# Linear attention with a mixture of depths: TensorE's warm-up in 32 products of 192 columns instead of 12 of 512, each fill of 512 columns as two of 256

## The chip, the cores and the metric

The kernel runs on one core of a Trainium2 chip. The metric is the device time of one execution in microseconds, as the median of several runs. The trace is of one execution that the hardware profiler recorded.

## The reference

Eight batches of eight heads go through an attention whose softmaxes are taken separately over q's features and over k's sequence. The result feeds a layer that picks 128 of 576 rows per batch by a score, sends them through two matrix products with a relu between, and adds them back, scaled by a gate.

```python
def _attn_ref(q, k, v):                      # each (8, 8, 576, 64): B, H, S, D
    q_s = np.exp(q - np.max(q, axis=-1, keepdims=True))
    q_s = q_s / (np.sum(q_s, axis=-1, keepdims=True) + 1e-09)
    k_s = np.exp(k - np.max(k, axis=2, keepdims=True))
    k_s = k_s / (np.sum(k_s, axis=2, keepdims=True) + 1e-09)
    kv = np.einsum('bhsd,bhse->bhde', k_s, v)
    return np.einsum('bhsd,bhde->bhse', q_s, kv)
# x: the result as (B, S, H*D) = (8, 576, 512); w1 (512, 1024), w2 (1024, 512), capacity 128
def _moe_ref(x, w_gate, w1, w2, capacity):
    scores = np.einsum('bsd,d->bs', x, w_gate)
    out = x.copy()
    for b in range(B):
        top_idx = np.argpartition(-scores[b], capacity)[:capacity]
        xe = x[b, top_idx]
        ye = np.maximum(xe @ w1, 0.0) @ w2
        g = 1.0 / (1.0 + np.exp(-scores[b, top_idx]))
        out[b, top_idx] = xe + g[:, None] * ye
    return out
```

## The kernel before, in words

The work of the attention is cut into 16 units: a unit is one batch and four of its eight heads. For a unit, `load` brings k, v and q to the core (three buffers each), `k_exp` and `q_exp` take exponentials on ScalarE, `v_copy` (L275) copies v beside a column of ones, `kv_mm` (L311; `kv_mm_parts`, L299, for unit 1) forms the products of exponentials and v on TensorE, `kv_out` (L319 to L323) divides them on VectorE, `q_t` (L340, L347) turns q by TensorE, with copies back to the core's memory at L350 and L352, and `x_mm` (L375, with fillers of bf16 at L364) forms the unit's rows x. `x_sums` and `x_scale` (L386 to L393) divide them and `x_store` writes them out.

For a batch, `score_row` (L432) spreads its scores, `compare` (L443) ranks them on VectorE, and the chosen rows go through the two products with w1 and w2: `mlp1` (L555) and `mlp2` (L564) for the first two batches, and for pairs of later ones a scheme with fewer products of half the size (L648, L704). Batch 0's rows are taken by products with a selection matrix (`select`, L504 to L509), the others by an indirect load.

The order of all of this is written out by hand: each engine executes its instructions in the order in which the kernel issues them, and the pieces of the two products are spread between the units (`pieces`, `upto`). Ahead of the first unit there is no work for TensorE while the first loads are under way.

In that place the kernel issues products that nobody reads, with `ones_b` (128x512 bf16 ones) as both operands. The warm-up (L174) is 12 products of 512 columns into one bank of the accumulation memory, right after VectorE has set `ones_b`. `fill(n)` (L854) issues n such products into a bank of the tag "mm". It is called four times, all at the head of the kernel: fill(1) after the products at L860, which spread w_gate, and ahead of `kv_mm(0)`; fill(3) between `kv_out(0)` and `q_t(0, 0)`; fill(1) ahead of `x_mm(0, 0)`; fill(1) ahead of `q_t(1, 1)`. Each product is two instructions of TensorE, a load of its stationary operand (PEld in the profile) and the product (PE). A product of two f32 operands is issued as two such pairs, and each of them is counted as one product in the profile.

At the end eight more products of the same kind stand (L1177), and a branch that skips a general path.

Of the kernel before, what the change touches and what calls it, by code (L numbers as in the profile page):

```python
# [17 lines left out]
def kernel(  # L18
# [23 lines left out]
    nc = tc.nc  # L42
    B, H, S, D = q.shape
    DM, F = moe_w1.shape
    P = 128
# [15 lines left out]
    NV = 5  # L61
    TURNED = frozenset((11, 13, 15))
    HC = 32
    WARM = 12
    assert S == 64 * T and D == 64 and DM == H * D and DM == 512 and H % 4 == 0
    assert 1 < capacity < S and KF == 8 and NQ == 2
    assert B * S <= 32 * 256
# [14 lines left out]
    def bank(tag, bufs):  # L82
        return ps.tile([P, 512], F32, tag=tag, name=tag, bufs=bufs)
# [84 lines left out]
    ones_b = const.tile([P, 4 * P], BF16, name="ones_b")  # L168
    nc.vector.memset(ones_b, 1.0)
    w_ps = bank("tp", 2)  # L170
    ones_f = const.tile([1, D], F32, name="ones_f")
    nc.vector.memset(ones_f, 1.0)
    for n in range(WARM):
        nc.tensor.matmul(out=w_ps, lhsT=ones_b[:, :P], rhs=ones_b, start=True, stop=True)  # L174
    warm = const.tile([P, 1], F32, name="warm")
    nc.scalar.activation(out=warm, in_=ones_b[:, :1], func=AF.Exp)
    ident = const.tile([P, P], F32, name="ident")
# [672 lines left out]
    def fill(n):  # L850

        junk_ps = bank("mm", 2)
        for _ in range(n):
            nc.tensor.matmul(out=junk_ps, lhsT=ones_b[:, :P], rhs=ones_b, start=True, stop=True)  # L854


    wg = const.tile([P, NQ, 2, D], F32, name="wg")
# [1 line left out]
    for h in range(2):  # L859
        nc.tensor.matmul(out=g_ps[part(h), :4 * D], lhsT=ones_f,  # L860
                         rhs=w_row.rearrange("o (n i x) -> o i n x", i=2, x=2 * D)[:, h], start=True, stop=True)
    fill(1)
    ready(0)
    nc.vector.tensor_copy(out=wg.rearrange("p a i d -> p (a i d)"), in_=g_ps[:, :4 * D])
    kv_mm(0)
    q_exp(0, 0)
    q_exp(0, 1)
    kv_out(0)
    fill(3)

    q_t(0, 0, on_vector=True)
# [6 lines left out]
    q_exp(1, 1)  # L878
    k_exp(1)
    fill(1)  # L880
    x_mm(0, 0)
    x_mm(0, 1)
# [323 lines left out]
```

## Time and profile before

| what | us |
|---|---|
| median of three runs | 198.19 |
| the three runs | 197.4, 198.19, 198.81 |
| the profiled execution | 197.7 |
| its span, first to last instruction | 195.8 |
| TensorE busy, products | 184.2 |
| VectorE busy | 130.4 |
| ScalarE busy | 99.7 |
| GpSimd busy | 72.7 |

Times in the profile are counted from the start of the span. A product's recorded duration holds its way through the engine, and products overlap, so the distance between the starts of two is what one costs in a run of them.

### The profile page before, as it was taken

What the parts mean: (1) busy time and instruction counts of PE and PEld (TensorE: products, weight loads), DVE (VectorE), ACT (ScalarE), POOL (GpSimd) and SP (SyncE); (2) the same over time, 40 slices, a digit from 0 to 9 for tenths busy, and PEclk for the clock granted to TensorE, in tenths of its full rate; (3) what the DMA queues carried; (4) which work ended last, traced back from release to release, by engine and by line L of the source; (5) the groups of instructions that cost most, each with busy time, mean ns of one, the idle gap of its engine ahead of it and who ended that gap; (6) DMA issues with size and microseconds to landing.
All of it is one profiled execution on the core that took longest, in us unless ns stands there. A gap on an engine that the chain in (4) does not pass through costs nothing.

```text
span 195.8 us, 7049 instructions
## 1 busy us (share of the span) xinstructions
PE 184.2 (94%) x2927; PEld 156.0 (80%) x2927; DVE 130.4 (67%) x429; ACT 99.7 (51%) x160; POOL 72.7 (37%) x131
## 2 busy tenths in 40 slices
PE   5798899999999999999999999999999999999990
PEld 2466699894679996769999888899998889898860
DVE  6377966494669749928978989489959955444010
ACT  3474625658199759938675759365423133312100
POOL 8013551100860392099682312242314354701230
PEclk9999999999999999999999999999999999999997
DMA  5999999999999999989999799989451514010011
GB/s 153 364 365 378 378 368 364 328 388 352 341 379 374 336 314 363 308 248 152 312 325 320 130 317 330 273 160 257 158 121 57 121 38 149 32 54 5 3 56 63
DMA packets 48361, 46.67 MB, mean 238 GB/s; under 512 B 16321, under 2 KB 41921, under 8 KB 48322
## 3 DMA queue, kind: packets, MB, share of 16 engines
q1 hardware_dynamic: 46768, 41.62, 67.4%
q0 software_dynamic: 1280, 4.20, 6.7%
q8 instruction: 25, 0.41, 0.9%
q10 hardware_dynamic: 274, 0.33, 0.5%
q14 instruction: 14, 0.11, 0.2%
HBM read 34.61 MB, written 11.53 MB: 236 GB/s over the span
## 4 chain that ended last, share of the span: by engine, by line
PE 85%; DVE 6%; DMA 3%; issue 1%; ACT 1%; POOL 1%; POOLq 0%; DVEq 0%
PE mm L704 19%; PE mm L648 18%; PE tp L311 10%; PE x L375 10%; PE mm L555 8%; PE mm L564 8%; PE x L347 4%; DMA v<-in_v_dram 3%; PE mm L509 2%; PE tp L432 2%; PE x L530 2%; DVE xs L393 1%; DVE v_ones L280 0%; PE tp L468 0%; DVE v_ones L275 0%
## 5 line engine op out<-in xcount | busy, mean ns | idle before, releaser
L443 DVE SCALAR_TENSOR_TENSOR junk<-srow,s,stairs 128x576 bf16<-128x576 f32 x40 | 33.4, 834 | 1.5 <-ACT srow L435 0.8
L393 DVE TENSOR_TENSOR xs<-x,qrec 128x640 f32<-128x640 f32 x32 | 25.2, 815 | 0.0
L375 PE MATMUL x<-kv_w,qT 64*64 64x66 f32 x1152 | 23.2, 222 | 1.2 <-issue 0.5
L375 PEld LDWEIGHTS x<-kv_w,qT 64*64 64x64 f32 x1152 | 20.7, 134 | 4.5 <-issue 2.1
L352 ACT COPY qT<-x 128x512 f32<-128x512 f32 (+1 forms) x24 | 14.3, 643 | 17.1 <-PE x L347 16.6
L311 PE MATMUL tp<-v_ones,ke 128*64 128x65 f32 x600 | 21.6, 224 | 1.4 <-DVE v_ones L275 1.1
L704 PE MATMUL mm<-w,hT 128*128 128x256 f32 x96 | 22.2, 379 | 0.0
L249 ACT ACTIVATE ke<-k 128x1280 f32<-128x1280 f32 x16 | 20.4, 1274 | 3.4 <-issue 1.4
L311 PEld LDWEIGHTS tp<-v_ones,ke 128*64 128x64 f32 x600 | 19.2, 137 | 3.6 <-issue 1.9
L493 POOL DMA_INDIRECT xr<-out_dram,idx x8 | 8.1, 1018 | 36.3 <-DVE no L486 9.8
L704 PEld LDWEIGHTS mm<-w,hT 128*128 128x128 f32 x96 | 17.8, 190 | 2.2
L257 ACT ACTIVATE qe<-q 128x640 f32<-128x640 f32 (+1 forms) x26 | 16.4, 683 | 5.7 <-DMA q<-in_q_dram 3.0
L704 PE MATMUL mm<-tw,hT 128*128 128x256 f32 (+1 forms) x80 | 17.6, 363 | 0.0
L648 PE MATMUL mm<-xT,w 128*128 128x128 f32 x144 | 17.5, 276 | 0.0
L275 ACT COPY v_ones<-v 128x1280 f32<-128x1280 f32 x12 | 15.1, 1258 | 3.8 <-PE tp L311 2.5
L648 PEld LDWEIGHTS mm<-xT,w 128*128 128x128 f32 x144 | 16.8, 192 | 0.1
L555 PE MATMUL mm<-xT,w 128*128 128x128 f32 x128 | 16.7, 281 | 0.0
L713 POOL TENSOR_TENSOR o<-o,xr 128x256 f32<-128x256 f32 x9 | 6.8, 757 | 23.6 <-ACT o L712 23.6
L564 PE MATMUL mm<-w,hT 128*128 128x512 f32 x32 | 15.6, 611 | 0.0
L555 PEld LDWEIGHTS mm<-xT,w 128*128 128x128 f32 x128 | 15.0, 191 | 0.5
L704 PEld LDWEIGHTS mm<-tw,hT 128*128 128x128 f32 x80 | 13.8, 190 | 2.0 <-DVE o L717 0.4
L386 DVE RECIPROCAL qrec<-x 128x10 f32<-128x10 f32 x32 | 7.0, 217 | 12.6 <-PE x L375 12.2
(162 smaller groups left out, 311.2 us busy)
## 6 DMA issues: line engine op xcount, KB each, us to landing
q<-in_q_dram SPq DMA_DIRECT2D x26, 288.0 KB, 5.7
v<-in_v_dram SPq DMA_DIRECT2D x16, 320.0 KB, 5.4
out_dram<-xs SPq DMA_DIRECT2D x16, 320.0 KB, 5.6
k<-in_k_dram SPq DMA_DIRECT2D x15, 320.0 KB
k<-in_k_dram SPq DMA_DIRECT2D x16, 256.0 KB, 5.9
v<-in_v_dram SPq DMA_DIRECT2D x16, 256.0 KB
out_dram<-xs SPq DMA_DIRECT2D x16, 256.0 KB, 4.8
w<-in_moe_w_dram SPq DMA_DIRECT2D x4, 512.0 KB, 8.2
```

Source lines behind the costliest of these rows:

```text
L249: nc.scalar.activation(out=ke, in_=raw["k"][u % LD], func=AF.Exp)
L257: nc.scalar.activation(out=st["qe", u][:, r0:r1], in_=qr[:, r0:r1], func=AF.Exp)
L275: copy(out=v_ones[:, :, :, :D], in_=raw["v"][u % LD])
L311: nc.tensor.matmul(out=kv[part(h), i], lhsT=ke[:, 2 * h + i, r], rhs=vo[:, 2 * h + i, r], start=(r == 0), stop=(r == N2))
L352: nc.scalar.copy(out=to, in_=src)
L375: nc.tensor.matmul(out=to[:, r * C:(r + 1) * C], lhsT=lhsT, rhs=kw[part(i), a], start=True, stop=True)
L393: nc.vector.tensor_mul(xs[b][:, :, qd, :, a].rearrange("p r i d -> p i r d"), x[:, :, :, :D], rec.to_broadcast([P, 2, R, D]))
L443: nc.vector.scalar_tensor_tensor(junk, st["srow", b], st["s", b][:, r:r + 1], not_before[r], op0=OP.subtract, op1=OP.is_ge, accum_out=st[" ...
L555: nc.tensor.matmul(out=h_ps[:, f % HT * m:(f % HT + 1) * m], lhsT=w1[:, d, f * P:(f + 1) * P], rhs=xT[:, d, :m], start=(d == 0), stop=(d = ...
L564: nc.tensor.matmul(out=st["y", b][:m], lhsT=st["hT", b][:, f // HT, f % HT, :m], rhs=w2[:, f], start=(f == 0), stop=(f == KF - 1))
L648: nc.tensor.matmul(out=out_ps[:, f * m:(f + 1) * m], lhsT=w[:, k, f * P:(f + 1) * P], rhs=x()[:, k], start=first and f == 0 and k == 0, st ...
L704: nc.tensor.matmul(out=ps_of[to][:m, c:c + step], lhsT=st["hT", a][:, n, f, :m], rhs=w[:, f, c:c + step], start=first and f == 0, stop=f = ...
```

## The change

`WARM` is 32 instead of 12, and each of these products has 192 columns instead of 512: 6,144 columns in either case. `fill(n)` issues 2n products of 256 columns instead of n of 512. In all there are 20 products more in the warm-up and 6 more in the fills, 26 products or 52 instructions. Nothing else differs.

```diff
--- before.py
+++ after.py
@@ -61,7 +61,7 @@
     NV = 5
     TURNED = frozenset((11, 13, 15))
     HC = 32
-    WARM = 12
+    WARM = 32
     assert S == 64 * T and D == 64 and DM == H * D and DM == 512 and H % 4 == 0
     assert 1 < capacity < S and KF == 8 and NQ == 2
     assert B * S <= 32 * 256
@@ -171,7 +171,7 @@
     ones_f = const.tile([1, D], F32, name="ones_f")
     nc.vector.memset(ones_f, 1.0)
     for n in range(WARM):
-        nc.tensor.matmul(out=w_ps, lhsT=ones_b[:, :P], rhs=ones_b, start=True, stop=True)
+        nc.tensor.matmul(out=w_ps[:, :192], lhsT=ones_b[:, :P], rhs=ones_b[:, :192], start=True, stop=True)
     warm = const.tile([P, 1], F32, name="warm")
     nc.scalar.activation(out=warm, in_=ones_b[:, :1], func=AF.Exp)
     ident = const.tile([P, P], F32, name="ident")
@@ -850,8 +850,8 @@
     def fill(n):
 
         junk_ps = bank("mm", 2)
-        for _ in range(n):
-            nc.tensor.matmul(out=junk_ps, lhsT=ones_b[:, :P], rhs=ones_b, start=True, stop=True)
+        for _ in range(2 * n):
+            nc.tensor.matmul(out=junk_ps[:, :2 * P], lhsT=ones_b[:, :P], rhs=ones_b[:, :2 * P], start=True, stop=True)
 
 
     wg = const.tile([P, NQ, 2, D], F32, name="wg")
```

## Rows read from the trace of the kernel before

**Rows 1.** The page: part 1's line of TensorE (busy us, share of the span, instructions; loads are PEld), part 3's line of its instruction queue (packets, MB, share of 16 engines), and part 4, the chain that ended last, by engine.

```profile
PE 184.2 (94%) x2927; PEld 156.0 (80%) x2927; DVE 130.4 (67%) x429; ACT 99.7 (51%) x160; POOL 72.7 (37%) x131
...
q8 instruction: 25, 0.41, 0.9%
...
PE 85%; DVE 6%; DMA 3%; issue 1%; ACT 1%; POOL 1%; POOLq 0%; DVEq 0%
```

**Rows 2.** The chain of work that ended last, in order of time, from 2 to 11 us: start us, us, what, and how many instructions.

```profile
2.32 5.13 DMA v<-in_v_dram
...
7.54 0.84 DVE v_ones L275
...
8.51 1.39 PE tp L311 x40
9.90 0.75 PE mm L854 x3
10.65 0.47 PE x L347 x10
```

**Rows 3.** The timeline of TensorE's products from 0 to 13 us, instructions of one kind merged: start us, us until the last one ends, then in brackets the idle time before and what ended it.

```profile
2.07 4.45 PE L174 MATMUL tp<-ones_b 128*128 128x512 bf16 x12 [2.07 <-DVE second_p L182]
6.45 0.65 PE L860 MATMUL tp<-w_row,ones_f 1*64 1x256 f32 x4
7.03 0.39 PE L854 MATMUL mm<-ones_b 128*128 128x512 bf16 x1
8.51 1.39 PE L311 MATMUL tp<-v_ones,ke 128*64 128x65 f32 x40 [1.09 <-DVE v_ones L275]
9.83 0.82 PE L854 MATMUL mm<-ones_b 128*128 128x512 bf16 x3
10.58 0.77 PE L347 MATMUL x<-ident,qe 64*128 64x64 f32 x18
...
12.03 0.73 PE L375 MATMUL x<-kv_w,qT 64*64 64x66 f32 x33 [0.35 <-DVE qT L350]
```

**Rows 4.** The table by stretches: us from the span's start, length, then busy time and instructions of PE, PEld, DVE, ACT and POOL, the granted clock, the DMA share and GB/s.

```profile
2.00:4.00 2.00, 1.93 (x5) 0.74 (x6) 1.64 (x13) 1.17 (x1) 1.93 (x5) 1.00 0.73 211
```

**Rows 5.** Line L174, the warm-up: its loads with their duration (ns min/median/max), and single loads and a product from the timeline (start us, us).

```profile
L174 PEld LDWEIGHTS <-ones_b x12: 97/152/152, 2.1 to 5.9; 128*128 128x128 bf16 x12
...
5.04 0.15 PEld L174 LDWEIGHTS <-ones_b 128*128 128x128 bf16 x1 [0.28 <-issue]
5.46 0.56 PEld L174 LDWEIGHTS <-ones_b 128*128 128x128 bf16 x3 [0.27 <-issue]
...
5.93 0.10 PEld L174 LDWEIGHTS <-ones_b 128*128 128x128 bf16 x1
...
6.14 0.38 PE L174 MATMUL tp<-ones_b 128*128 128x512 bf16 x1
```

**Rows 6.** What one product costs: two long stretches of the chain (36 products of 256 columns, 64 of 128; start us, us), and the five loads of 128x128 bf16 at L477, whose products have 5 columns, together in the timeline.

```profile
150.22 8.04 PE mm L704 x36
...
167.15 7.38 PE mm L648 x64
...
29.23 0.19 PEld L477 LDWEIGHTS <-hit 128*128 128x128 bf16 x5
```

**Rows 7.** The chain in order of time: the pieces called issue that lie inside TensorE's work: the four longest, and one short one.

```profile
17.16 0.23 issue
...
23.63 0.39 issue
...
36.31 0.25 issue
...
50.31 0.06 issue
...
138.36 0.14 issue
```

**Rows 8.** The table by stretches with the columns of rows 4, cut where TensorE resumes after the stops called issue: first from one such point to the next, then from the start to one of them and to two earlier points. In brackets behind the second and the third time are the numbers of products and of loads.

```profile
17.37:24.01 6.64, 5.45 (x125) 4.62 (x126) 5.35 (x15) 3.57 (x7) 4.20 (x11) 1.00 1.05 382
24.01:36.55 12.54, 12.29 (x252) 11.64 (x252) 6.85 (x30) 6.29 (x8) 3.30 (x5) 1.00 1.04 355
36.55:138.48 101.93, 101.67 (x1905) 85.52 (x1904) 78.13 (x256) 68.16 (x108) 42.52 (x75) 1.00 0.98 300
...
0.00:24.01 24.01, 18.71 (x345) 12.58 (x346) 16.50 (x66) 12.47 (x18) 8.98 (x27) 1.00 0.94 327
...
0.00:15.93 15.93, 12.26 (x194) 7.21 (x196) 10.01 (x44) 8.16 (x11) 4.78 (x16) 1.00 0.88 300
0.00:20.63 20.63, 16.29 (x320) 10.62 (x322) 13.47 (x58) 9.85 (x13) 7.09 (x24) 1.00 0.92 319
```

**Rows 9.** The timeline from 15 to 31 us: start us, us, what, and in brackets the idle time before.

```profile
16.70 0.46 PE L375 MATMUL x<-kv_w,qT 64*64 64x66 f32 x15 [0.23 <-DVE krec L286]
...
20.22 0.80 PE L311 MATMUL tp<-v_ones,ke 128*64 128x65 f32 x20
...
21.61 0.77 PE L340 MATMUL x<-ident,qe 128*128 128x128 f32 x5 [0.58 <-ACT qe L257]
...
22.69 0.94 PE L509 MATMUL mm<-hT,xs 128*128 128x128 f32 x6
...
25.09 0.29 DVE L504 TENSOR_TENSOR hT<-slot_no,rank 128x128 f32<-128x128 f32 x1
```

## The prediction

> **What bounds the kernel now.** I read the page's share of the chain first, then the chain in order of time, then TensorE's timeline. TensorE is busy 94% of the span and carries 85% of the chain that ended last [rows 1]; from about 24 us on, its queue is full and nearly everything that delays it delays the end. Ahead of that the chain runs through a load: the first v lands at 7.45, VectorE copies it until 8.38, and only then does TensorE begin the first kv products, at 8.51 [rows 2]. The warm-up and the first fill lie beside that wait: TensorE is through with them at 7.42 and stands idle for 1.09 us [rows 3]. So the reader is to see two different places in one edit: the warm-up and fill(1) at 7.03 have a cover, and fill(3) at 9.83 has none, since the chain steps from L311 through L854 into L347 [rows 2]. The third call, fill(1) after the transposes, is covered again: the L375 products behind it wait 0.35 us for VectorE's qT [rows 3]. The fourth lies between x_mm and the transposes of unit 1.
>
> **The clock at the start.** The granted clock stands at 1.00 in the first stretches [rows 4], yet eight warm-up products follow each other at 0.43 us (5.04, 5.46, and so back to the first: 8 x 0.42 us is the 3.39 from 2.07 to 5.46), which is 512 columns at 1.2 GHz, and the later ones at 0.21 (5.93, 6.14), which is 2.4 GHz [rows 5]. I trust the spacings: TensorE ran at the lower level from 2.07 to 5.46, with products back to back, and then rose.
>
> **The warm-up.** The columns are the same, 6,144. If a weight load hides behind the product before it, as it does at 512 columns (it takes 0.15 us of 0.43 [rows 5]), the lower level fits 3.39 / 0.16 = 21 products of 192 columns, and the other 11 take 0.08 each: the end stays at 6.45. What does one more product cost by itself? In long stretches 36 products of 256 columns take 8.04 us, 223 ns each, and 64 of 128 columns take 7.38 us, 115 ns each [rows 6]. Two halves therefore cost 231 ns where one whole costs 223: some 7 ns for the extra pair of instructions. The upper bound is a bf16 load of 128 columns with a product of 5, where nothing hides anything: five loads take 0.19 us in all [rows 6], one takes 0.10 [rows 5], so they follow at 24 ns, 48 at half the clock. With that, a cold product takes 0.208 us, 16 of them fit into 3.39 us, and 16 more at 0.104 end at 7.1 instead of 6.45. The four L860 products and fill(1) still end by about 8.1, ahead of 8.51. Cost: nothing on the path, at either bound; the cover is the landing of v. If the cover were gone, it would be 0.14 us (20 x 7 ns) to 0.7 us.
>
> **The fills.** fill(3) is six products of 256 for three of 512: 3 x 7 = 0.02 us, upper bound 3 x 24 = 0.07. From the first of the three to L347 there are 0.75 us [rows 3]; two distances of 0.21 [rows 5] leave 0.32 from the last one to L347, where a product takes 0.21. If that 0.32 is a fixed delay from the start of the last product, the shorter last product cannot shrink it, and fill(3) grows by up to 0.1. So the bounds are 0 and 0.17; I take 0.02, the long stretches being the nearest rows. The first and the third call cost nothing, by their covers; the fourth has one pair more, 0.01 at most 0.02.
>
> **The 52 instructions as a shift.** This is where I expect the only visible effect. The chain has four stops of TensorE called issue, in the middle of runs of equal products, with nothing waited for: 0.23 at 17.16, 0.39 at 23.63, 0.25 at 36.31 and 0.14 at 138.36 [rows 7]. Between the instructions at which it resumes stand 251, 504 and 3,809 products and loads [rows 8], which are 1, 2 and 15 lots of 251 to 254 (waits of the sequencer are not in these counts). A cause tied to the data would not keep to such a lattice: I read them as points at equal counts of TensorE's instruction stream, and the page's instruction queue moves in 25 transfers of 0.41 MB, some 16 KB each [rows 1]. The Trainium skill, Runtime: NRT & Kernel Launch, section Instruction fetch mechanics, says that engines refill their instruction memory in blocks of 256 instructions; the counts agree with it.
>
> If so, all stops come 52 instructions earlier in the work than before. I look each up by its count:
> - The second stood at 345 + 346 = 691; 639 is close to 20.63, where the count is 642 [rows 8]. That is within the second half of kv_mm(2), L311, which ends some 0.6 us before the transposes L340, and these wait 0.58 us for ScalarE's qe [rows 9]. So 0.39 us leaves the path. What is late next: the products of L509 need VectorE's hits, of which the fourth is finished at 25.38 [rows 9]; without the stop TensorE, eight products for each hit and 0.115 us a product from 22.69 on, would want it at 25.45, so the feed just about keeps up. I take -0.39, bounds -0.45 and 0.
> - The first stood at 691 - 251 = 440; 388 is at 15.9, where the count is 390 [rows 8]: in L299, the kv products of unit 1. The L375 products behind them wait at 16.70 for VectorE's krec [rows 9], which reads what L299 makes. Either VectorE's own queue hides the stop there (-0.23), or krec comes late by as much as TensorE had stood still before (0). A longer stop there would be a loss: I take 0, bounds -0.23 and +0.16, the difference to the longest.
> - The third and the fourth move by 26 products too, in or just ahead of the run of short products in which they stood; I have no reason for another price and take 0 for each. They are worth 0.39 together [rows 7].
> - 5,854 products and loads [rows 1] hold some 23 such points; nineteen showed no stop of size, and each may get one. A shift by 26 products leaves most of them in a run of the same kind as before, so I don't take the rate of 4 in 23 for all of them, but one new stop of 0.25 at 4 chances in 10: +0.1. Bounds: 0, and two of the largest, 0.78.
>
> **The sum.** The profiled execution took 197.7 us, span 195.8 and 1.9 around it. 0 + 0.02 - 0.39 + 0 + 0.1 gives about -0.3, so 197.4. The median of the runs is 198.19, 0.49 above this execution; on that footing the forecast is 197.9.
>
> **Rivals.** (a) Nothing moves: the shift is worth zero because the stops are hidden in most executions or reappear at the same price. For it: 19 of 23 points had none. Then 198.2. The same section of the Trainium skill says that crossing a block is mostly hidden; by it the sum would lose the -0.39 and stand at 198.3, and the trace disagrees at four places, with 0.14 to 0.39 us. (b) Stops get worse: the new points fall where TensorE has little queued, as in the short products of L311 at 50.3, where a trace of one is seen already (0.06 [rows 7]). Two stops of 0.39 more and none less: 198.2 + 0.8 = 199.0. (c) Slower: 192-column products do not raise the clock as 512-column ones did. Place: L174, up to the first L311. It decides if products still come at the half rate when L311 starts at 8.51. Up to there the cover holds even then (32 x 0.16 ends at 7.19, the L860 products and the fill at about 8.7). From then on the chain's TensorE pieces up to 11.15 double: 1.39 + 0.75 + 0.47 = 2.6 us more [rows 2], and 0.2 for the late start: 201.0. Against it: weights load in 0.15 us at the lower level and a product of 192 takes 0.16, so nothing should open a gap. (d) The edit does not do what it says: the repeated load of equal weights might be left out by the build. In the trace each product has its own load (12 and 12 [rows 3, 5]), so I give this little; it would give 198.2 as in (a).
>
> **How the numbers follow.** Forecast 0.45, (a) with (d) 0.30, (b) 0.15, (c) 0.06, and 0.04 for a larger gain from a cause that I don't see (all four stops together hold only 1.0 us). The runs of before lie between 197.4 and 198.81, so 1%, or 2 us, is about what a measurement tells from no change. The range: down by all four stops from 198.2 and 0.5 for the spread, 196.7; up to (b) and a little spread, 199.2; (c) is left out. Faster by over 1% (under 196.2) is that last case: 0.04. Slower by over 1% (over 200.2) is (c) and little else: 0.07. Within 1%: 0.89.
>
> **What would show it.** Right: 32 L174 products at 0.16 and later 0.08 us, ending near 6.45; L311 still starting about 8.5 after v; L854 at 9.83 with six products in about 0.75 us; no issue stop inside L509, and L509's last start some 0.4 us nearer to L340's. Stops, where there are any, again at counts 251 to 254 apart, 52 earlier in the work. Wrong: L174 at 0.2 us or more with L311 later than 8.5; the stop still inside L509 at the same product; half-rate spacings after 8.5.

## The result, and the profile after

| | before | changed |
|---|---|---|
| median, 23 runs each | 198.94 us | 200.36 us |
| all runs | 197.33 to 201.84 | 198.6 to 205.49 |
| ratio | | 1.0062, 95% interval 1.0034 to 1.0089 |

The medians are of all executions, while every ratio here leaves out those of either kernel that fell into a slower state. The change costs some 1.2 us where 0.3 us of gain was forecast, and 200.36 lies above the range of 196.7 to 199.2. The profiled execution of the changed kernel took 204.06 us, well above its median, so the losses in it are larger than the usual ones; the profile of the third experiment below, at 200.7 us, shows the same places at a more usual size.

The page of the changed kernel: span, busy times, the granted clock by slices, and the chain by engine.

```profile
span 202.2 us, 7101 instructions
...
PE 186.7 (92%) x2953; PEld 161.6 (80%) x2953; DVE 130.6 (65%) x429; ACT 99.3 (49%) x160; POOL 73.0 (36%) x131
...
PEclk9999759999999999999999999999999999999998
...
PE 81%; DVE 9%; issue 3%; DMA 3%; ACT 1%; POOLq 0%; POOL 0%; DVEq 0%
```

TensorE has more to do by 2.5 us only, and its share of the chain falls from 85% [rows 1] to 81%, while issue rises from 1% to 3% and VectorE from 6% to 9%. The clock line has a dip in the fifth and sixth slice, from 20.2 to 30.3 us. The start is as the prediction had it, in the timeline of TensorE's products (start us, us, idle before):

```profile
2.08 4.53 PE L174 MATMUL tp<-ones_b 128*128 128x192 bf16 x32 [2.08 <-DVE second_p L182]
6.54 0.65 PE L860 MATMUL tp<-w_row,ones_f 1*64 1x256 f32 x4
...
8.63 1.39 PE L311 MATMUL tp<-v_ones,ke 128*64 128x65 f32 x40 [1.13 <-DVE v_ones L275]
9.95 0.83 PE L854 MATMUL mm<-ones_b 128*128 128x256 bf16 x6
10.71 0.77 PE L347 MATMUL x<-ident,qe 64*128 64x64 f32 x18
...
20.08 0.68 PE L311 MATMUL tp<-v_ones,ke 128*64 128x65 f32 x14
23.03 0.59 PE L311 MATMUL tp<-v_ones,ke 128*64 128x65 f32 x6 [2.27 <-issue]
23.55 1.33 PE L340 MATMUL x<-ident,qe 128*128 128x128 f32 x5
```

The warm-up of 32 ends at 6.54 where 12 had ended at 6.45 [rows 3]; L311 waits for v at 8.63, with 1.13 us to spare; the six products of fill(3) take 0.76 us to L347 where the three took 0.75. The loss is in the last rows. L311's second half stops after 14 of 20 products and goes on 2.27 us later. TensorE's waits name this stop and a second one:

```profile
PE tp L432 <- issue: 2.4, 1, 2.4
PE tp L311 <- issue: 2.3, 1, 2.3
```

Here is the table by stretches (length, products and loads in brackets, the granted clock third from the end), cut where TensorE goes on after these two stops and after a wait of 0.9 us in L468 (put down to VectorE's L393), and from the start to the first of them:

```profile
16.34:23.02 6.68, 4.26 (x126) 3.56 (x126) 5.51 (x20) 3.12 (x5) 3.52 (x10) 0.98 1.05 384
23.02:78.80 55.78, 53.34 (x1010) 45.26 (x1010) 33.92 (x128) 31.69 (x48) 20.09 (x36) 0.94 1.01 338
78.80:107.29 28.49, 27.57 (x509) 22.03 (x509) 21.61 (x68) 20.88 (x33) 15.34 (x21) 1.00 0.89 248
...
0.00:23.02 23.02, 16.82 (x346) 13.88 (x347) 15.77 (x64) 11.29 (x16) 8.30 (x26) 0.99 0.93 327
```

Between the resumptions stand 252, 2,020 and 1,018 products and loads: 1, 8 and 4 lots of 252 to 255, as in [rows 8]. The first resumption is at count 346 + 347 = 693, where before the stop in L509 stood at 691 [rows 8]. The same count of the stream lies 26 products earlier in the work, in L311. So the stops are where I put them, but one that was to vanish has grown sixfold. What follows it, with the two other pieces of the chain that matter (start us, us, what):

```profile
23.00:27.00 4.00, 3.97 (x26) 3.40 (x26) 3.86 (x15) 1.18 (x2) 2.73 (x4) 0.50 1.07 366
...
25.50 6.61 PE mm L509 x40
...
77.78 1.03 issue
```

After the stop the granted clock of 23 to 27 us is 0.50, the 1.2 GHz level; TensorE had stood still for 2.27 us. L509's 40 products take 6.61 us, most of them at that level (0.50 until 29 us, 0.86 from 29 to 31), where the kernel before took 5.2 us with a stop of 0.39 us among them (from 22.69 [rows 9] to L375 at 27.90). At 77.78 the next long stop is on the chain for 1.03 of its 2.4 us; the rest of it lies beside VectorE's work.

### The profile page after: what moved, and what is told of

It reads as the page before. It is cut to its first block, busy times and chain, and to the rows that moved or that the text cites. A ratio compares the mean times of both kernels' runs of the same rounds, so it can differ in the third digit from the quotient of the medians.

```text
span 202.2 us, 7101 instructions
## 1 busy us (share of the span) xinstructions
PE 186.7 (92%) x2953; PEld 161.6 (80%) x2953; DVE 130.6 (65%) x429; ACT 99.3 (49%) x160; POOL 73.0 (36%) x131
## 4 chain that ended last, share of the span: by engine, by line
PE 81%; DVE 9%; issue 3%; DMA 3%; ACT 1%; POOLq 0%; POOL 0%; DVEq 0%
PE mm L704 18%; PE mm L648 16%; PE x L375 10%; PE tp L311 9%; PE mm L564 7%; PE mm L555 7%; PE x L347 4%; PE mm L509 3%; DMA v<-in_v_dram 3%; PE tp L432 2%; DVE junk L443 2%; DVE xs L393 2%; PE x L530 1%; PE tp L299 1%; PE x L340 1%
## 5 line engine op out<-in xcount | busy, mean ns | idle before, releaser
L393 DVE TENSOR_TENSOR xs<-x,qrec 128x640 f32<-128x640 f32 x32 | 25.2, 815 | 0.0
L311 PE MATMUL tp<-v_ones,ke 128*64 128x65 f32 x600 | 21.5, 225 | 3.4 <-issue 2.3
L352 ACT COPY qT<-x 128x512 f32<-128x512 f32 (+1 forms) x24 | 14.3, 644 | 20.5 <-PE x L347 17.3
L311 PEld LDWEIGHTS tp<-v_ones,ke 128*64 128x64 f32 x600 | 19.1, 138 | 5.4 <-issue 4.0
L375 PEld LDWEIGHTS x<-kv_w,qT 64*64 64x64 f32 x1152 | 20.5, 134 | 3.6 <-issue 1.0
L375 PE MATMUL x<-kv_w,qT 64*64 64x66 f32 x1152 | 23.0, 222 | 0.5 <-DVE qT L350 0.3
L257 ACT ACTIVATE qe<-q 128x640 f32<-128x640 f32 (+1 forms) x26 | 16.4, 686 | 5.3 <-DMA q<-in_q_dram 2.7
```

The source lines that it names most:

```text
L257: nc.scalar.activation(out=st["qe", u][:, r0:r1], in_=qr[:, r0:r1], func=AF.Exp)
L311: nc.tensor.matmul(out=kv[part(h), i], lhsT=ke[:, 2 * h + i, r], rhs=vo[:, 2 * h + i, r], start=(r == 0), stop=(r == N2))
L352: nc.scalar.copy(out=to, in_=src)
L375: nc.tensor.matmul(out=to[:, r * C:(r + 1) * C], lhsT=lhsT, rhs=kw[part(i), a], start=True, stop=True)
L393: nc.vector.tensor_mul(xs[b][:, :, qd, :, a].rearrange("p r i d -> p i r d"), x[:, :, :, :D], rec.to_broadcast([P, 2, R, D]))
```

## The experiments

Theory A is that TensorE's instructions come in lots of some 253 products and loads, that a lot arrives a certain time after the one ahead of it was entered, and that the change only moves the ends of the lots. Theory B blames the 192-column warm-up, theory C the halved fills. All ratios are to the kernel before.

### One part of the change alone, and the count alone

The warm-up alone:

```diff
-    WARM = 12
+    WARM = 32
-        nc.tensor.matmul(out=w_ps, lhsT=ones_b[:, :P], rhs=ones_b, start=True, stop=True)
+        nc.tensor.matmul(out=w_ps[:, :192], lhsT=ones_b[:, :P], rhs=ones_b[:, :192], start=True, stop=True)
```

> The kernel before with the warm-up of 32 products of 192 columns and the fills left at 512: 40 more instructions of TensorE. Theory A (the instruction stream comes in lots of some 253 and a lot that arrives late stops TensorE; the change moves the ends of the lots): the stops move by 40, the first long one to the transposes L340 or just ahead of them, where TensorE waits for ScalarE anyway; ratio to before 0.995 to 1.008, the stops at counts 40 earlier than in the kernel before. Theory B (the 192-column warm-up itself costs, by a later rise of the clock): all of the loss is here, ratio 1.006. Theory C (the halved fills cost, on the chain at fill(3)): ratio 1.000.

Measured: 1.0061 (1.0022 to 1.0099), median 200.0 us. One long stop called issue, now ahead of the transposes L340, as the shift by 40 has it:

```profile
PE x L340 <- issue: 2.6, 1, 2.6
```

By the ratio alone this run speaks for B as much as for A.

The fills alone:

```diff
-        for _ in range(n):
-            nc.tensor.matmul(out=junk_ps, lhsT=ones_b[:, :P], rhs=ones_b, start=True, stop=True)
+        for _ in range(2 * n):
+            nc.tensor.matmul(out=junk_ps[:, :2 * P], lhsT=ones_b[:, :P], rhs=ones_b[:, :2 * P], start=True, stop=True)
```

> The kernel before with each fill of 512 columns as two of 256 and the warm-up left as it was: 12 more instructions of TensorE. Theory A: the stops move by 12 only, ratio 0.992 to 1.002, not the loss of the change. Theory B: ratio 1.000. Theory C: all of the loss is here, ratio 1.006.

Measured: 0.9975 (0.9939 to 1.0011). C falls: the halved fills, which lie on the chain, cost nothing that can be seen. The stop is in L509 again, 1.0 us. The profile puts it down to VectorE's hT, but it stands at the count of the lot's end, 691, and the first hT was finished at 22.09, 1.6 us before TensorE went on:

```profile
PE mm L509 <- DVE hT L504: 1.0, 1, 1.0
```

The count alone, without a product of another size:

```diff
-    def fill(n):
+    def fill(n, short=0):
         ...
+        for _ in range(short):
+            nc.tensor.matmul(out=junk_ps[:, :8], lhsT=ones_b[:, :P], rhs=ones_b[:, :8], start=True, stop=True)
...
-    fill(1)
+    fill(1, short=26)
     ready(0)
```

> The kernel before with its own products, and 26 more products of 8 columns behind the first fill(1), where TensorE stands idle for 1.09 us (26 x 24 ns = 0.62 us): 52 more instructions, as in the change, but no product of another size. Theory A: the same as the change, ratio 1.003 to 1.009, and the same stops: about 2.3 us in L311 near 20.5 us, 2.4 us in L432 near 76 us, 0.9 us in L468 near 106 us. Theories B and C: ratio 1.000, stops as in the kernel before.

Measured: 1.0119 (1.0074 to 1.0163). The same warm-up and the same fills as before, and the loss is there, at least as large as the change's. The waits show the change's places, L311, L432 (put down to VectorE's L522) and L468:

```profile
PE tp L311 <- issue: 2.2, 1, 2.2
...
PE tp L432 <- DVE g L522: 1.3, 1, 1.3
...
PE tp L468 <- issue: 0.2, 1, 0.2
```

and between the resumptions the same counts of 126 and 126, 1,010 and 1,010, 509 and 509:

```profile
16.36:23.01 6.65, 4.27 (x126) 3.54 (x126) 5.46 (x20) 3.12 (x5) 3.52 (x10) 1.00 1.02 353
23.01:76.21 53.20, 51.86 (x1010) 43.79 (x1010) 33.87 (x128) 31.68 (x48) 19.96 (x36) 0.97 1.03 349
76.21:103.95 27.74, 27.56 (x509) 22.03 (x509) 21.12 (x69) 20.88 (x33) 14.73 (x21) 1.00 0.92 268
```

The clock falls behind the first stop here too, from 23 to 27 us, in an execution of 200.7 us:

```profile
23.00:27.00 4.00, 3.98 (x28) 3.42 (x28) 3.86 (x15) 1.18 (x2) 2.74 (x4) 0.57 1.07 376
```

B falls as an explanation of the change: no warm-up of smaller products is needed for it. (32 products of 192 columns at a count that costs nothing were not run.) Why 26 short products cost 1.0119 and the change 1.0062 isn't settled; the intervals overlap.

About half of them, with `short=12`:

> The kernel before with 12 more products of 8 columns in the same idle place: 24 more instructions. Theory A: by the times that the lots took in the trace of before, the stops now fall in cheaper places: ratio 0.992 to 1.000, and stops at counts 24 earlier than in the kernel before. Theories B and C: ratio 1.000.

Measured: 1.0015 (0.9977 to 1.0054). No difference is seen; the expected gain didn't come. The stop is shorter and lies in L347:

```profile
PE x L347 <- issue: 0.6, 1, 0.6
```

### More and fewer, and the smaller products at a cheap count

With `short=46`:

> The kernel before with 46 short products in the idle place behind the first fill(1) (46 x 24 ns = 1.10 us in 1.09 us): 92 more instructions, no product of another size. Theory A, with each lot entered no sooner than about 5 to 6.8 us after the one ahead of it, as seen at the stops so far: stops of about 3 us near 19 us, 1 us near 57, 2.5 us near 75 and 1.9 us near 105, some 3 us more in sum than with 26 short products: ratio to before 1.015 to 1.035. If what costs is the number of short products themselves, 46 cost 46/26 of the 1.0119 of e3_26_short: 1.021. If neither: 1.000.

Measured: 1.0197 (1.0116 to 1.0278). Two long stops, 3.4 us ahead of L432 near 20 us and 1.9 us in L375 near 75.6 us; the stops of 1 us near 57 and 1.9 near 105 didn't come.

```profile
PE tp L432 <- issue: 3.4, 1, 3.4
PE x L375 <- issue: 2.1, 2, 1.9
```

The rival by number had 1.021, so the ratio doesn't tell the two apart; the stops do: they begin eleven and more us behind the last short product, at counts 692 and 2,711, where the lots of the changed kernel end too (693 and 2,713).

With `short=6`:

> The kernel before with 6 short products in the same place: 12 more instructions, the smallest sum of stops by the same count (2.8 us where before has 4.6 and the change 7.1). Theory A: ratio 0.990 to 0.999, one stop of some 1.2 us near 23 us in L509 or L347 and little else. If what costs is the number of short products themselves: 1.003. If neither: 1.000.

Measured: 0.9984 (0.9938 to 1.003). One stop, 1.0 us in L509, and little else, but no gain that stands out:

```profile
PE mm L509 <- DVE hT L504: 1.0, 1, 1.0
```

The same count of 12 more instructions through a finer warm-up:

```diff
-    WARM = 12
+    WARM = 18
-        nc.tensor.matmul(out=w_ps, lhsT=ones_b[:, :P], rhs=ones_b, start=True, stop=True)
+        nc.tensor.matmul(out=w_ps[:, :341], lhsT=ones_b[:, :P], rhs=ones_b[:, :341], start=True, stop=True)
```

> The kernel before with a warm-up of 18 products of 341 columns (6,138 columns in all) and its fills as they were: 12 more instructions and smaller products in the warm-up. Theory A: like e7_6_short and e2_fills_only, ratio 0.990 to 1.000. Theory B (smaller products in the warm-up cost): between 1.000 and 1.006, about 1.002.

Measured: 0.9986 (0.9945 to 1.0026). Six more products in the warm-up cost nothing; together with the fills alone (also 12 instructions) these are three ways to the same count and three ratios from 0.9975 to 0.9986. In its profiled execution v came late, L311 began at 9.24 after 1.55 us of idling, and the clock of 10 to 12 us was at 0.50:

```profile
9.24 2.29 PE L311 MATMUL tp<-v_ones,ke 128*64 128x65 f32 x40 [1.55 <-DVE v_ones L275]
...
10.00:12.00 2.00, 1.67 (x30) 1.61 (x28) 0.40 (x3) 0.98 (x2) 0.00 (x0) 0.50 1.08 383
```

That is a second place where the level falls, behind the wait for v. It came once more, with 32 products of 192 columns (e9_change_swap below, 1.32 us of idling), and not behind 1.24 us of idling with the same products (e5_less_dma); no execution with 12 products of 512 idled longer than 1.10 us there, so the length of the wait and the size of the products aren't told apart.

### Why a lot is late

The changed kernel with less for the DMA engines to move:

```diff
     load(2, "vq")
-    load_w1(0)
-    load_w1(1)
...
-    load(3, "kvq")
...
-    load(4, "kvq")
-    load_w2(0)
-    load_w2(1)
...
     x_store(2)
+    load_w1(0)
+    load_w1(1)
+    load_w2(0)
+    load_w2(1)
```

> The changed kernel without the loads of k, v and q for units 3 and 4 (these units compute on what units 0 and 1 left in the buffers), and with the loads of w1 and w2 issued only behind the store of unit 2. Around 16 to 23 us little is left for the DMA engines to move. Same instructions of TensorE. Only the stop near 20.5 us is looked at; the whole time says nothing. Theory A with a lot that is late because its transfer waits behind data: the instruction queue's transfer that ends about 1.3 us ahead of the resumption starts within 2 us of the lot before it being entered (16.4 us), not 4.3 us after, and the stop of 2.3 us is under 0.5 us or gone. Rival A2 (a lot takes its 6.7 us whatever the DMA engines carry, or the stop is a fixed price for a crossing): a stop of 2 us or more stays.

Measured: the stop is gone. The second half of L311 runs through its 20 products, L340 waits 0.58 us for ScalarE as in [rows 9], and L509 takes 4.97 us without a stop, while the DMA engines have 3 GB/s to move from 18 to 22 us:

```profile
19.95 0.80 PE L311 MATMUL tp<-v_ones,ke 128*64 128x65 f32 x20
21.33 0.77 PE L340 MATMUL x<-ident,qe 128*128 128x128 f32 x5 [0.58 <-ACT qe L257]
...
22.42 4.97 PE L509 MATMUL mm<-hT,xs 128*128 128x128 f32 x40
...
18.00:22.00 4.00, 3.13 (x65) 2.47 (x54) 3.29 (x9) 1.90 (x5) 2.44 (x10) 1.00 0.01 3
```

The instruction queue's transfer for the lot starts between 17.6 and 17.7 us (queue 8 has none from 16.1 to 17.6):

```profile
q8 instruction: 1, 0.02, 69.3%
```

In the changed kernel it starts between 20.6 and 20.7, with none from 16.4 to 20.6:

```profile
q8 instruction: 1, 0.02, 69.9%
```

So 1.6 us instead of 4.3 after the lot ahead was entered. This lot in the table by stretches, each from its entry to the entry of the next (length; GB/s is the last column; a row also counts instructions that straddle its cuts), in the kernels of e1_warm_only, e4_12_short, e6_46_short, e9_change_swap and, last, e5_less_dma:

```profile
16.60:23.55 6.95, 4.06 (x132) 3.39 (x128) 6.00 (x21) 3.12 (x5) 3.88 (x11) 1.00 1.01 346
```

```profile
17.02:23.51 6.49, 4.60 (x127) 3.82 (x126) 4.73 (x16) 3.57 (x6) 3.50 (x10) 1.00 1.04 379
```

```profile
15.93:23.48 7.55, 3.35 (x127) 2.98 (x127) 4.03 (x16) 1.36 (x2) 2.67 (x9) 0.99 1.02 366
```

```profile
17.42:23.95 6.53, 4.02 (x134) 3.42 (x130) 5.55 (x21) 3.12 (x5) 3.52 (x10) 1.00 0.89 299
```

```profile
16.04:20.34 4.30, 3.97 (x124) 3.41 (x125) 3.37 (x14) 1.67 (x2) 2.29 (x8) 1.00 0.32 114
```

With 299 to 384 GB/s of data beside it this lot takes 6.49 us or more in the first four of these, whatever it holds; 6.64 in the kernel before [rows 8], 6.68 in the changed one, 6.65 with 26 short products, and 6.1 to 6.2 in the last two runs below. With 114 GB/s it takes 4.30 us, and TensorE doesn't stop. A2 falls. The time is no constant under load either: a later lot of the changed kernel (counts 1,702 to 1,955) was over in 5.7 us without a stop of its own:

```profile
53.77:59.47 5.70, 5.70 (x134) 3.72 (x130) 3.15 (x13) 3.11 (x4) 2.65 (x3) 1.00 1.02 341
```

The last three runs ask if another order of the loads helps, the four of w1 behind those of unit 3:

```diff
     load(2, "vq")
-    load_w1(0)
-    load_w1(1)
...
     load(3, "kvq")
+    load_w1(0)
+    load_w1(1)
```

> The changed kernel with the four loads of w1 (512 KB each, 8.2 us to landing where loads of k, v and q take 5.4 to 5.9) issued behind those of unit 3 instead of ahead of them. TensorE's instructions are those of the change. Theory A, with a lot that waits behind the data queued before it: around 16 to 21 us shorter transfers lie ahead of it, so the stop near 20.5 us shrinks from 2.3 us to about 1, and the ratio falls from the change's 1.006 to about 1.000. If the wait doesn't depend on which loads are queued: the stop stays at 2.2 to 2.3 us and the ratio at 1.003 to 1.009.

Measured: 1.0078 (1.0035 to 1.012), and the stop is as long as before:

```profile
PE tp L311 <- issue: 2.2, 1, 2.2
```

So in the changed kernel the order of the loads made no difference to the stop; that part of my expectation fell. Behind the wait for v, of 1.32 us, the clock is low in this profile as well:

```profile
10.00:12.00 2.00, 2.00 (x25) 1.61 (x23) 0.86 (x6) 0.56 (x2) 0.00 (x0) 0.50 1.07 369
```

> The kernel before with the same swap of loads. It shows what the swap alone is worth: by theory A the stops of 0.23 and 0.39 us at 17 and 23.6 us shrink or go, ratio 0.995 to 1.000; if the loads of unit 3 or w1 are waited for anywhere, above 1.000.

Measured: 0.9973 (0.9928 to 1.0019), not to be told from no difference. In its profile the two stops are gone, as expected (0.05 us is left of the first). The transfer starts at 20.35, 2.9 us after the entry at 17.40 and not 4.1 as in the kernel before (21.47 after 17.38), and TensorE goes through the lot without a stop:

```profile
17.40:23.61 6.21, 5.40 (x126) 4.65 (x127) 4.94 (x14) 3.67 (x7) 3.75 (x11) 1.00 1.00 324
```

Why the swap moved the transfer here and not in the changed kernel is open.

> The kernel before with 6 short products (e7_6_short) and the swap. Theory A: the one stop of 1.04 us that e7_6_short has left, in L509, shrinks or goes: ratio 0.990 to 0.998. Otherwise as e7_6_short, 0.998.

Measured: 0.9994 (0.9951 to 1.0038). No gain. The stop in L509 shrank to 0.8 us, but there are new ones, 1.0 us in L375 until 18.2 and 1.5 us in L375 near 110:

```profile
PE x L375 <- issue: 2.6, 3, 1.5
...
18.23:24.36 6.13, 4.70 (x125) 4.03 (x126) 4.89 (x14) 2.93 (x6) 3.74 (x11) 1.00 1.05 362
```

No version here beats the kernel before by more than its interval.

## Why the prediction was wrong

- The warm-up and the clock's first rise: right. 32 products of 192 ended 0.09 us later than 12 of 512, under the cover of v; rival (c) didn't come, and theory B wasn't needed. The moment of the rise differs from one execution to the next whatever the size: in e1_warm_only all 32 products follow each other at 160 ns, the lower level, and the warm-up of 12 in e11_6_short_swap is as long:

```profile
2.08 5.30 PE L174 MATMUL tp<-ones_b 128*128 128x192 bf16 x32 [2.08 <-DVE second_p L182]
```

```profile
2.08 5.30 PE L174 MATMUL tp<-ones_b 128*128 128x512 bf16 x12 [2.08 <-DVE second_p L182]
```

- The fills: right. 0.76 for 0.75 us at fill(3), and 0.9975 for the fills alone.
- The 52 instructions as a shift: the place was right to a few counts, the price was wrong, and this is the step that failed. I took the second stop as a fixed price of 0.39 us paid at a point, and so as lost in the 0.58 us that L340 waits anyway, a term of -0.39. It is the rest of a wait: with data queued the next lot comes 6.1 to 7.6 us after this one was entered (the rows above), and TensorE stops for as long as it gets there sooner. Moved by 26 products, the lot holds L299's, L375's and L311's short products and no longer L340's wait for ScalarE and the first products of L509. TensorE gets through it in 4.4 us (16.34 to 20.76) instead of 6.3 (17.37 to 23.63), so the stop grows by about the difference, from 0.39 to 2.27 us. I had the length of the lot in [rows 8], 6.64 us for 251 instructions, and did not ask how short a lot may be.
- What then runs late: I asked only what hides the stop, not what it does to the clock. The stop of 2.27 us was followed by 0.50 of the clock, and L509 took 6.61 us in that execution where it took 4.97 without a stop (e5_less_dma), some 1.6 us more.
- The first stop: nothing speaks against the place and the price of 0. It stands in L299, at 16.11 to 16.35 us, and L375 behind it no longer waits 0.23 us for krec.
- The other lots: +0.1 was taken for new stops, bounds 0 and 0.78. L432 alone had 2.4 us of idling in the changed kernel's profile, 1.3 with 26 short products. The bound came from the largest stop seen, and a stop has no such bound.
- Rival (b) had the right sign and mechanism's name, 199.0, with a chance of 0.15; it too took 0.39 for the largest price.

What the runs leave open: how the usual 1.2 us divides between the stop near 20.5 us, the clock behind it and the stop near 76 us, since each kernel has one profile and the stops differ from one execution to the next. The profile doesn't show what starts a lot's transfer. That the later stops also come from lots that wait for data was not tried by itself. They stand at the same counts, and a transfer of the instruction queue ends ahead of them as it does ahead of the first. In the changed kernel, in the stretches 76.5 to 76.6 and 105.0 to 105.1 us:

```profile
q8 instruction: 1, 0.02, 60.4%
```

```profile
q8 instruction: 1, 0.02, 58.4%
```

One packet of 60.4% of 16 engines in 0.1 us is 0.97 us long, the other 0.93, so they end at 77.5 and 106.0, and TensorE goes on at 78.80 and 107.29, 1.3 us later. In all traces here the stops of 0.5 us or more that are called issue or stand in L509 end 1.2 to 1.5 us after such a transfer.

## What to carry to other kernels

Where TensorE goes through many short products while the DMA engines are full, its own instructions can come late: count the products and loads between stops that nothing explains, and if the counts are multiples of one number, the time from one such point to the next is what must not be short (here, under 6.1 us for the lot at 17 to 24 us). An edit that adds a few instructions, wherever it is hidden, moves all later ends of lots, so it is to be judged against a control with the same count, and the work that falls into each lot is to be timed anew. A stop of TensorE costs more than its length where the clock falls behind it.

## What was not expected of the hardware

The lots' transfers: 4.3 us from a lot's entry to the start of the transfer under 384 GB/s of data, 1.6 us where little was queued, and 1.2 to 1.5 us from its end to TensorE's resumption. In the changed kernel its one packet of 69.9% of 16 engines in 0.1 us is 1.12 us long, so it ended near 21.8, and TensorE went on at 23.03.

The clock: two stops of the same length, 1.0 us at the same place, were followed by different levels. First the fills alone, then 6 short products, from 23 to 27 us:

```profile
23.00:27.00 4.00, 3.29 (x16) 3.29 (x16) 3.86 (x15) 0.55 (x2) 2.74 (x4) 0.59 1.08 366
```

```profile
23.00:27.00 4.00, 3.63 (x33) 3.63 (x33) 3.69 (x15) 0.21 (x1) 2.62 (x4) 1.00 1.07 365
```

At 0.59 of the clock 16 products went through in 4 us, at 1.00 there were 33. Some of the spread between executions of one kernel may come from this; that wasn't measured.
